# A new step order, engine choice and PSUM bank table for an RWKV-6 recurrence followed by a token-mixing MLP

## The chip, the cores and the metric

The kernel runs on one core of one Trainium2 chip. The metric is the device time of one execution in microseconds (us). Before the change three runs gave 100.65, 100.91 and 101.37 us, a median of 100.91 us.

## The reference

Shapes: batch 4, 8 heads, 768 tokens, 48 columns per head, so 384 model columns; 64 hidden columns in the mixer. Inputs and output are float32.

```python
for t in range(S):                                   # for each of 4 x 8 heads
    y[:, :, t] = r_t @ (state + (u * k_t) (x) v_t)   # (x): outer product, 48 x 48
    state = w_t[:, None] * state + k_t (x) v_t
x = y as [B, S, H * D]
W_tok = (x @ w_q) @ (x @ w_k).T / 8                  # per batch, 768 x 768, no softmax
out = relu(W_tok @ x) @ w_out
```

The kernel never forms `W_tok`: it forms T = (x w_k)^T x (64 x 384) once per batch and multiplies by (x w_q), so the mixer of a batch waits for all of that batch's tokens.

## The kernel before

**Units.** The work is cut into 12 units of 256 tokens (three per batch, n = 0 to 11), each of two chunks c = 0, 1 of 128 tokens. `unit` (L382) adds the steps of one unit to a plan. For each unit four loads of 384 KB (`wg`, `kg`, `rg`, `vg`; for the last batch v comes in four loads `vw`) go through SyncE's queue into rings of four buffers. Unit n, by the names used below, in order of dependence:

- `ln` (L407, ScalarE): log of w; `cw`: its running sum, on TensorE; `ep`, `en` (L447, L454, ScalarE): exponentials of it, read from the same PSUM buffer.
- `k16`, `r16`, `v16` (L418, L421, L543): casts to bf16; `kT`, `rT`: transposes on TensorE into one PSUM buffer of two banks; `ks` (L502): copy of the transposed k; `qT` (L506), `RT` (L516): products read from the transposed r, always on VectorE; `KT` (L519): from `ks` and `en` on GpSimd (way P), from the same on VectorE (D), or from the PSUM buffer and `en` on VectorE (d).
- `vp`, `VB` (L555): v in the chunk's row order; for the last batch `VB` is a copy from `vw` (L537). `dps`, `dd`: the bonus with u; `Vd` (L575, GpSimd) = VB times dd.
- `A` (TensorE) and `AM` (L595, VectorE, one per chunk): masked scores; `kb`, `kd`: k by rows; `sn` (TensorE) and `SB` (L658, VectorE): the state, passed from chunk to chunk.
- `yi`, `ya` (TensorE): the state's and the scores' part of y; `X` (L710, in the last unit L715, VectorE): y plus Vd, the mixer's input; `xt`, `XT`: its transpose; `qk`, `QK`: the hidden columns. The last unit does this by chunk (`wq`, `wk`).
- After a batch's third unit: `T`, `TS`; then for each of the three units `mx` (TensorE), `rl` (relu into tile MX, L339 or L341), `fp` (TensorE, w_out), `os` (copy to an output tile, L327 or L333), `st` (store, SyncE's queue L841).

In the profile nearly all copies have line L327 (ScalarE) or L333 (VectorE, GpSimd), scaled ones L329 or L335, and every matmul has line L179. A step on TensorE is a run of 3 to 16 pairs of one weight load and one matmul.

**What sets the order.** Nothing is scheduled at run time. Three tables at the top of the file decide: `ORDER` (L82) gives the sequence in which the 734 steps are written out, and so each engine's own instruction order; `WAYS` (L124) gives one letter for each step that has a choice of engine or form (P GpSimd, D or d VectorE, A ScalarE; E, e, c forms on TensorE); `BANKS` (L129) gives the first of the eight PSUM banks for each PSUM buffer. `Plan.order` (L61) applies them. Each engine runs its steps strictly in that order and waits by semaphores for what a step reads, for the buffer it overwrites, and, where VectorE and ScalarE read the same PSUM banks, for the reader that was written out first. Twelve `z` steps are idle matmuls on zeros, also placed by the table.

Of the kernel before, what the change touches and what calls it, by code (L numbers as in the profile page):

```python
# [32 lines left out]
class Plan:  # L33
# [46 lines left out]


ORDER = [  # L82
# [40 lines left out]
]  # L123
WAYS = (  # L124
    "PDDDAPPDDdPADPPDDEEEAAPPAdPAAPEAcEEAAPPAPPADPeDEEDAAAAAAAAPPDPDADPeAcEEDAPPAdPAAPEAEEEDA"
    "PPDPPAAPeAEEAAAAAAAAAAPDPPAAPEDEcEAAPPDPPDAPEAEEEAAPPDPPAAPeDceAAAAADADDPAAPPAPEDcEEDAPP"
    "DPPAPeAcceAAPPDPPPAPPAEEDDAEDADAAADAAAADADDA"
)
BANKS = [  # L129
# [6 lines left out]
]  # L136


# [755 lines left out]
```

## Time and profile before

| | |
|---|---|
| median of 3 runs | 100.91 us (100.65 to 101.37) |
| span of the profiled execution | 99.6 us |
| median less span | 1.31 us |
| VectorE busy | 84.9 us of the span |
| ScalarE busy | 79.0 us |
| TensorE matmul busy | 86.6 us |
| GpSimd busy | 69.5 us |
| read from HBM, written | 19.66 MB, 4.72 MB |

The profiled execution is known by its span alone, the time from its first to its last recorded instruction; what lies around the span is taken as the 1.31 us between it and the median. Busy times are of instructions that run; matmuls overlap, so a busy TensorE is not one at its peak. In rows of the timeline the first number is the start, the second the duration, and a bracket at the end gives the idle time before the row and what ended it. "issue" as the thing that ended a wait means that no semaphore did.

### The profile page before, as it was taken

Reading aid. Unit: us, or ns where it says so; the run is one execution under the profiler, and the core shown is the slowest. Engines: PE = TensorE matmul, PEld = TensorE weight load, DVE = VectorE, ACT = ScalarE, POOL = GpSimd, SP = SyncE. Lnnn points to the kernel's source line nnn. Section 1 sums busy time; section 2 is a strip of 40 time slices with the busy share of each in tenths; the row PEclk is TensorE's granted clock in tenths of the full one; section 3 lists DMA queues with packets and bytes.
Section 4 is the critical chain, followed back from the end, with each engine's and each line's share of the span. In section 5 each row is a group of like instructions: output and inputs, shape, how many; then the busy total and the mean of one; then the engine's idle time right before and its main releaser. Section 6 shows DMA issues by size and latency. Waiting matters only on the chain.

```text
span 99.6 us, 4492 instructions
## 1 busy us (share of the span) xinstructions
PE 86.6 (87%) x1906; PEld 63.3 (64%) x1911; DVE 84.9 (85%) x154; ACT 79.0 (79%) x135; POOL 69.5 (70%) x82
## 2 busy tenths in 40 slices
PE   5978796879886998999999999889998999999930
PEld 1325473756774767777776777759787687776610
DVE  6284999799979999979999999999999799783740
ACT  6034998799996799899999998999899766666920
POOL 6866354999799895799999989498996392500000
PEclk9999999999999999999999999999999999999999
DMA  1999999799999999999999977998993056030794
GB/s 17 313 327 349 324 337 296 195 295 335 289 314 298 225 311 329 344 321 268 271 330 305 316 114 218 251 156 201 282 417 115 7 210 264 10 158 7 277 367 149
DMA packets 45141, 24.68 MB, mean 248 GB/s; under 512 B 31552, under 2 KB 43968, under 8 KB 45120
## 3 DMA queue, kind: packets, MB, share of 16 engines
q1 hardware_dynamic: 44960, 24.19, 84.0%
q8 instruction: 15, 0.25, 0.9%
q10 hardware_dynamic: 160, 0.20, 0.5%
q14 instruction: 6, 0.05, 0.1%
HBM read 19.66 MB, written 4.72 MB: 245 GB/s over the span
## 4 chain that ended last, share of the span: by engine, by line
PE 37%; DVE 23%; SPq 20%; DMA 7%; issue 7%; ACT 3%; ACTq 0%; DVEq 0%
PE PS L179 37%; SPq L232 9%; SPq L237 8%; DMA vg<-in_v_dram 7%; DVE AM L595 7%; DVE X L710 6%; DVE RT L516 3%; SPq L355 2%; DVE qT L506 2%; DVE ks L333 2%; DVE SB L658 1%; ACT VB L327 1%; SPq L357 1%; ACT MX L339 1%; DVE kd L335 1%
## 5 line engine op out<-in xcount | busy, mean ns | idle before, releaser
L595 DVE TENSOR_TENSOR AM<-PS,US 128x1024 bf16<-128x1024 f32 x24 | 28.8, 1218 | 0.7 <-PE PS L179 0.7
L526 POOL TENSOR_TENSOR KT<-ks,en 128x1024 bf16<-128x1024 bf16 (+1 forms) x10 | 19.7, 1965 | 4.7 <-DVE ks L333 3.3
L575 POOL TENSOR_TENSOR Vd<-VB,dd 128x768 bf16<-128x768 bf16 (+1 forms) x14 | 18.1, 1293 | 4.5 <-ACT dd L327 3.4
L454 ACT ACTIVATE en<-PS 128x1024 bf16<-128x1024 f32 (+1 forms) x14 | 12.5, 907 | 3.0 <-PE PS L179 2.9
L179 PEld LDWEIGHTS <-KT 48*128 48x128 bf16 (+1 forms) x312 | 9.7, 94 | 6.6 <-issue 4.5
L447 ACT ACTIVATE ep<-PS 128x512 bf16<-128x512 f32 (+1 forms) x28 | 13.7, 555 | 0.1
L179 PE MATMUL PS<-wo,MX 128*128 128x384 bf16 x72 | 13.5, 327 | 0.0
L710 DVE SCALAR_TENSOR_TENSOR X<-PS,gx,Vd 128x384 bf16<-128x384 f32 x22 | 12.5, 609 | 0.7 <-PE PS L179 0.6
L407 ACT ACTIVATE lw<-wg 128x768 bf16<-128x768 f32 x12 | 10.3, 857 | 2.9 <-DMA wg<-in_w_dram 2.9
L179 PE MATMUL PS<-RT,KT 48*128 48x128 bf16 x192 | 9.7, 218 | 1.2 <-ACT VB L327 0.4
L327 ACT COPY os<-PS 128x768 f32<-128x768 f32 (+1 forms) x11 | 7.9, 714 | 3.5 <-PE PS L179 3.5
L418 POOL CAST k<-kg 128x768 bf16<-128x768 f32 x10 | 8.3, 827 | 2.5 <-DMA kg<-in_k_dram 2.5
L179 PE MATMUL PS<-Z 128*128 128x512 bf16 x25 | 8.4, 461 | 1.4 <-DVE Z L250 1.2
L418 POOL CAST r<-rg 128x768 bf16<-128x768 f32 x10 | 8.2, 825 | 1.6 <-DMA rg<-in_r_dram 1.6
L179 PEld LDWEIGHTS <-MX 128*128 128x128 bf16 x72 | 6.5, 97 | 3.6 <-DVE MX L341 0.2
L516 DVE TENSOR_TENSOR RT<-PS,ep 128x1024 bf16<-128x1024 bf16 (+1 forms) x14 | 8.4, 605 | 0.0
L179 PE MATMUL PS<-VB,AM 128*128 128x48 bf16 x192 | 8.0, 184 | 0.4 <-issue 0.4
L506 DVE TENSOR_TENSOR qT<-PS,ks 128x1024 bf16<-128x1024 bf16 x12 | 8.2, 684 | 0.1
L339 ACT ACTIVATE MX<-PS 128x768 bf16<-128x768 f32 (+1 forms) x12 | 8.0, 682 | 0.4
L179 PE MATMUL PS<-CM,lw 64*128 64x128 bf16 x192 | 7.4, 217 | 0.5 <-DVE AM L595 0.3
L327 ACT CAST VB<-PS 128x768 bf16<-128x768 f32 x8 | 6.4, 804 | 1.1 <-PE PS L179 0.6
L179 PEld LDWEIGHTS <-AM 128*128 128x128 bf16 x192 | 6.3, 96 | 1.6 <-issue 0.7
(90 smaller groups left out, 191.9 us busy)
## 6 DMA issues: line engine op xcount, KB each, us to landing
kg<-in_k_dram SPq DMA_DIRECT2D x12, 384.0 KB, 6.4
wg<-in_w_dram SPq DMA_DIRECT2D x12, 384.0 KB, 5.0
rg<-in_r_dram SPq DMA_DIRECT2D x12, 384.0 KB, 5.8
vg<-in_v_dram SPq DMA_DIRECT2D x9, 384.0 KB, 6.3
out_dram<-os SPq DMA_DIRECT2D x9, 384.0 KB, 2.5
vw<-in_v_dram SPq DMA_DIRECT2D x4, 288.0 KB, 6.7
out_dram<-os SPq DMA_DIRECT2D x5, 192.0 KB, 2.4
wof<-in_moe_w_out_dram SPq DMA_DIRECT2D x1, 576.0 KB, 6.2
```

Of the source, the lines that this page charges most:

```text
L179: return nc.tensor.matmul(o, l, rr, start=start, stop=stop, skip_group_check=True, is_transpose=trans)
L327: nc.scalar.copy(o, i)
L407: nc.scalar.activation(view(lw.tile, 0, [[64, H], [512, 2], [1, D]]), view(g["wg"].tile, 0, [[D2, H], [D, 2], [1, D]]), ACT.Ln, bias=0.0, ...
L418: op(view(o.tile, 0, [[64, NP], [256, 4], [1, D]]), view(g[src].tile, 0, [[2 * D2, NP], [D, 4], [1, D]]))
L447: nc.scalar.activation(view(ep.tile, cs[0] * NP * EW + off, [[EW, NP * len(cs)], [step, 2], [1, 32]]), view(at(cw), cs[0] * 512 + j * 64, ...
L454: nc.scalar.activation(en.tile[:, ds(cs[0] * 512, w_)], at(cw)[:, ds(cs[0] * 512, w_)], ACT.Exp, bias=0.0, scale=-1.0)
L506: lambda e: nc.vector.tensor_tensor(plain(qT.tile), turned(512), plain(ks.tile), ALU.mult),
L516: nc.vector.tensor_tensor(plain(RT.tile, cs, 32), turned(512, cs, True), plain(ep.tile, cs, EW // 4), ALU.mult)
L526: x.tensor_tensor(KT.tile[:, cols], ks.tile[:, cols], en.tile[:, cols], ALU.mult)
L575: (nc.vector if e == "D" else nc.gpsimd).tensor_tensor(Vd.tile[:, cols], VB.tile[:, cols], view(dd.tile, cs[0] * H, [[1, len(cs) * H], [0, ...
L595: AMs[c] = add(("AM", n, c), "D", lambda e, c=c, A=A: nc.vector.tensor_tensor(view(AM[c].tile, 0, [[C, 8], [1, C]]), view(at(A), 0, [[C, 8 ...
L710: nc.vector.scalar_tensor_tensor(view(X.tile, 2 * i * DM + hh * D, [[D2, H], [1, D]]), view(at(y), hh * 512, [[D, H], [1, D]]), gx, view(V ...
```

## The change

Only the three tables change. The functions, the operations and their operands are the same, and the numbers of buffers too. The description that comes with it: the order was searched with a model that lets two readers of a PSUM bank take turns and that holds TensorE's instruction blocks apart.

```diff
 ORDER = [
-    0, 3, 13, 2, 21, 22, 23, 15, 16, 17, 1, 24, 25, 26, 27, 28, 29, 76, 77, 78, 31, 73, 74, 75,
...
+    0, 1, 2, 3, 4, 24, 25, 26, 15, 16, 17, 32, 30, 33, 21, 22, 23, 31, 38, 39, 730, 13, 18, 19,
...
 WAYS = (
-    "PDDDAPPDDdPADPPDDEEEAAPPAdPAAPEAcEEAAPPAPPADPeDEEDAAAAAAAAPPDPDADPeAcEEDAPPAdPAAPEAEEEDA"
...
+    "PPPAAADDdPPADPPDDEEeAAPPAdPADPEAccEAAPPDPPAAPeAcEAAAAAAAAAPPAdPAAPEAEEEDAPPDPPAAPEAEEEAA"
...
 BANKS = [
-    7, 2, 0, 6, 0, 6, 4, 4, 1, 1, 6, 6, 5, 4, 2, 6, 0, 0, 0, 7, 7, 6, 4, 5, 4, 4, 2, 2, 7, 0, 0,
...
+    5, 0, 2, 0, 2, 4, 2, 0, 3, 3, 4, 0, 7, 4, 6, 6, 7, 2, 4, 2, 5, 5, 6, 7, 5, 0, 2, 6, 1, 2, 0,
...
```

Steps that change engine or form, by unit:

- from VectorE: `pads` 0 and 1 (zeroing `kd`), `v16` 3 to GpSimd; `uC`, `ks` 3, `VB` 7, `XT` 2 and 4, `kd` 2, 8 and 9, `dd` 2 and 3, `rl` 7 and 8 and some `os` to ScalarE; `KT` 4 and the second half of `KT` 0 to GpSimd (the first half of `KT` 0 goes from form D to form d);
- to VectorE: `r16` 0, `KT` 3 and 6 and the first half of `KT` 11 from GpSimd; `ks` 2, 4 and 9, `kd` 5, 7 and 11, `dd` 1, 6 and 9, `XT` 8, `QK` 7 and 9, `TS` 8 and 11, `rl` 9 and a half of `rl` 10 from ScalarE;
- between GpSimd and ScalarE: `k16` 0, `r16` 5, `v16` 8 and `VB` 9 go to ScalarE, `k16` 6 and `r16` 9 to GpSimd;
- on TensorE: four `kb` steps take the form with half as many matmuls, so 1887 pairs stand in the program instead of 1911.

The first loads were kg 0, wg 0, rg 0, vg 0, kg 1, wg 1, rg 1, vg 1 and so on; now they are rg 0, wg 0, kg 0, kg 1, wg 1, rg 1, vg 0, kg 2, wg 2, vg 1, rg 2, vg 2. The two small loads of w_q and w_k stood 13th and now come after rg 4, 18th.

The moved pieces at three places follow. A name is a tile with the ring slot and a running number.

**VectorE at the start of the program** (units 0 and 1; KT_0, RT_0, ks_0, ep_0 are unit 0's). Before:

```order
L297 MEMSET kd_0_83 128x32
L298 MEMSET kd_0_83 128x16x40
L297 MEMSET kd_1_84 128x32
L298 MEMSET kd_1_84 128x16x40
L333 CAST uC_134<-uR_133 8x128
L333 COPY ks_0_95<-PS_62 128x1024
L526 TENSOR_TENSOR KT_0_101<-ks_0_95,en_0_93 128x512
L521 TENSOR_TENSOR KT_0_101<-PS_62,en_0_93 128x512
L516 TENSOR_TENSOR RT_0_99<-PS_62,ep_0_91 128x512
L506 TENSOR_TENSOR qT_0_97<-PS_62,ks_0_95 128x1024
```

Now:

```order
L421 CAST r16_0_87<-rg_0_67 128x8x2x48
L333 COPY ks_0_95<-PS_62 128x1024
L521 TENSOR_TENSOR KT_0_101<-PS_62,en_0_93 128x512
L516 TENSOR_TENSOR RT_0_99<-PS_62,ep_0_91 128x512
L506 TENSOR_TENSOR qT_0_97<-PS_62,ks_0_95 128x1024
L595 TENSOR_TENSOR AM0_0_111<-PS_62,US_146 128x1024
L516 TENSOR_TENSOR RT_0_99<-PS_62,ep_0_91 128x512
L333 COPY dd_0_107<-PS_62 128x16
L335 TENSOR_SCALAR kd_0_83<-PS_62,gk_152 128x8x48 x2
L595 TENSOR_TENSOR AM1_0_113<-PS_62,US_146 128x1024
```

The memsets and the cast of uC are gone from VectorE, the cast of r is there, and the first AM follows right behind the first chunk's KT, RT and qT, ahead of kd.

**ScalarE ahead of the last unit's `ln`** (lw_1_86 from wg_3_66 is unit 11's, kd_0_83 is unit 10's, XT_0_119 is unit 8's). Before:

```order
L327 COPY os_3_82<-PS_62 128x768
L327 COPY XT_0_119<-PS_62 128x768
L327 CAST QK_0_127<-PS_62 128x384
L329 ACTIVATE kd_0_83<-PS_62,gk_152 128x16x48
L327 CAST QK_0_127<-PS_62 128x384
L407 ACTIVATE lw_1_86<-wg_3_66 128x8x2x48
```

Now:

```order
L327 COPY os_3_82<-PS_62 128x768
L329 ACTIVATE kd_0_83<-PS_62,gk_152 128x16x48
L339 ACTIVATE MX_0_121<-PS_62 128x768
L327 COPY dd_0_107<-PS_62 128x16
L327 CAST VB_1_106<-vw_0_131 128x8x2x48
L339 ACTIVATE MX_1_122<-PS_62 128x768
L407 ACTIVATE lw_1_86<-wg_3_66 128x8x2x48
```

Unit 9's VB, which GpSimd made, now stands in ScalarE's row behind kd, MX and dd, and the state step `sn` 9 on TensorE and `SB` 9 on VectorE wait for it; XT 8 and one QK have left.

**ScalarE in the last batch's mixer** (os_2_81 is unit 6's output tile and os_3_82 unit 7's; XT_0_119 is unit 10's; MX_0_121 is unit 8's). Before:

```order
L327 COPY XT_0_119<-PS_62 128x768
L327 COPY os_2_81<-PS_62 128x768
L327 CAST QK_1_128<-PS_62 128x384 x2
L327 CAST QK_1_128<-PS_62 128x128
L327 CAST QK_1_128<-PS_62 128x64
L327 CAST TS_1_130<-PS_62 128x384
L327 COPY os_3_82<-PS_62 128x768
```

Now:

```order
L327 COPY XT_0_119<-PS_62 128x768
L327 COPY os_3_82<-PS_62 128x768
L327 CAST QK_1_128<-PS_62 128x64
L327 CAST QK_1_128<-PS_62 128x384
L339 ACTIVATE MX_0_121<-PS_62 128x768
L327 COPY os_0_79<-PS_62 128x768
```

Unit 7's output (fp 7 on TensorE, then os 7) now precedes the last T and TS; before it followed them. TS 11 is on VectorE now. On TensorE the end reads: fp 8, mx 9, mx 10, mx 11, then fp 9, and the halves of fp 11 and fp 10 by turns; before it read fp 7, mx 9, fp 8, mx 10, fp 9, mx 11, fp 10, fp 11.

More of the change, by code (lines that the diff above doesn't have):

```diff
@@ L82 @@
 ORDER = [
[40 rows of a table removed]
[40 rows of a table added]
 ]
 WAYS = (
-    "PDDDAPPDDdPADPPDDEEEAAPPAdPAAPEAcEEAAPPAPPADPeDEEDAAAAAAAAPPDPDADPeAcEEDAPPAdPAAPEAEEEDA"
-    "PPDPPAAPeAEEAAAAAAAAAAPDPPAAPEDEcEAAPPDPPDAPEAEEEAAPPDPPAAPeDceAAAAADADDPAAPPAPEDcEEDAPP"
-    "DPPAPeAcceAAPPDPPPAPPAEEDDAEDADAAADAAAADADDA"
+    "PPPAAADDdPPADPPDDEEeAAPPAdPADPEAccEAAPPDPPAAPeAcEAAAAAAAAAPPAdPAAPEAEEEDAPPDPPAAPEAEEEAA"
+    "PADPPAAPEDEEAAAAAAAAAPPDdPADPEDcEEAAPPDPPAAPEDEEEADPPDPAAAPEAEEDADAAAAAAPPDPADPEAccEDDPP"
+    "DPPAPEAcEeAAPPDdPPAPPDEEDADEDDDDDDADADDDADAA"
 )
 BANKS = [
[6 rows of a table removed]
[6 rows of a table added]
 ]
```

88 rows, old and new, of tables (BANKS, ORDER) are left out of this document.

## The prediction

> **What bounds the kernel now.** I read the page's busy shares first, then busy time by stretch, then the timelines of VectorE, TensorE, ScalarE and GpSimd around each idle time of VectorE.
>
> ```profile
> span 99.6 us, 4492 instructions
> DVE  6284999799979999979999999999999799783740
> DMA  1999999799999999999999977998993056030794
> q8 instruction: 15, 0.25, 0.9%
> ```
>
> ```profile
> 6.00:27.00 21.00, 16.99 (x417) 11.99 (x419) 18.78 (x37) 17.29 (x30) 14.65 (x16) 1.00 1.07 307
> 27.00:36.00 9.00, 7.74 (x204) 6.13 (x203) 8.27 (x15) 7.21 (x11) 8.44 (x8) 1.00 0.99 276
> 36.00:75.50 39.50, 37.67 (x961) 29.48 (x960) 38.76 (x61) 38.27 (x64) 35.46 (x31) 1.00 1.01 277
> 75.50:85.60 10.10, 9.43 (x216) 6.85 (x217) 9.21 (x17) 6.66 (x16) 5.71 (x7) 1.00 0.33 125
> 85.60:95.60 10.00, 9.96 (x107) 7.01 (x108) 6.70 (x13) 6.97 (x15) 0.52 (x1) 1.00 0.38 145
> ```
>
> The columns of the second view are TensorE, weight loads, VectorE, ScalarE, GpSimd, granted clock, DMA share and GB/s. From 6.0 to 85.6 us, where the last AM ends, VectorE is busy 18.78 + 8.27 + 38.76 + 9.21 = 75.0 of 79.6 us: it sets the pace and is idle 4.6 us. ScalarE is nearly as full in the long middle (38.27 of 39.5). Behind 85.6 the last unit's mixer is a chain with TensorE in the lead. DMA is full early, so the first 30 us also hang on when loads land. So the span is 6.0 + VectorE's work up to the last AM + its idle time + the chain behind it, and I cost the change by these terms.
>
> ```profile
> 83.23 2.34 DVE L595 TENSOR_TENSOR AM<-PS,US 128x1024 bf16<-128x1024 f32 x2
> 86.24 1.14 DVE L715 SCALAR_TENSOR_TENSOR X<-PS,gx,Vd 128x384 bf16<-128x384 f32 x2 [0.67 <-PE PS L179]
> 94.23 0.56 DVE L341 TENSOR_SCALAR MX<-PS 128x384 bf16<-128x384 f32 x1 [0.73 <-ACT MX L339]
> ```
>
> ```profile
> 93.70 0.50 ACT L339 ACTIVATE MX<-PS 128x384 bf16<-128x384 f32 x1
> ...
> 95.64 0.48 ACT L327 COPY os<-PS 128x384 f32<-128x384 f32 x1 [0.98 <-PE PS L179]
> ```
>
> The chain from AM's end (85.57) to the last copy's end (96.12) takes 10.55 us, the last store and the close 3.5 us: 6.0 + 75.0 + 4.6 + 10.5 + 3.5 = 99.6. The median of the runs is 1.31 us above this span, and I add the same 1.31 to mine.
>
> **The work that moves.** Nothing is removed but 24 of 1911 pairs on TensorE, which is not the pace. What counts is how much VectorE must do before the last AM.
>
> ```profile
> L333 DVE COPY ks<-PS 128x1024 bf16<-128x1024 bf16 x8 | 5.5, 685 | 1.7 <-PE PS L179 1.7
> L327 ACT COPY ks<-PS 128x1024 bf16<-128x1024 bf16 x4 | 4.0, 1008 | 1.1 <-PE PS L179 1.1
> L521 DVE TENSOR_TENSOR KT<-PS,en 128x1024 bf16<-128x1024 bf16 x2 | 1.4, 678 | 0.0
> L333 DVE CAST v<-vg 128x768 bf16<-128x768 f32 x1 | 1.3, 1306 | 0.7 <-DMA vg<-in_v_dram 0.7
> L327 ACT CAST VB<-PS 128x768 bf16<-128x768 f32 x8 | 6.4, 804 | 1.1 <-PE PS L179 0.6 <-issue 0.4
> ```
>
> In a full row an instruction costs about 0.08 us less than its mean, since the next starts that much before its end: 0.60 for ks or KT, 1.23 for the cast. Off VectorE: pads and uC 1.6 (they run from 6.00 to 7.59, uC last, row below), the v cast 1.23, ks 3 and KT 4 1.2, three kd 1.56, two XT 0.94, VB 7 0.86, KT 0 0.6, two dd 0.2: 8.2. Onto it: the r cast 1.23, three ks 1.8, KT 3 and 6 1.2, kd 5 and 7 1.04, XT 8, QK 7 and TS 8 1.38, halves of KT 11 and kd 11 0.66, three dd 0.3: 7.6. So VectorE has 0.6 us less: 74.4. ScalarE, by the same count, has 1.9 us more to do up to the end of `ln` 11 (63.0 for 61.1); GpSimd loses over 2 us in all and is no bound (35.46 of 39.5 in the middle).
>
> **The start.** VectorE's idle times before 10 us are 0.94 and 0.38, waits for kT 0 and for en 0.
>
> ```profile
> 6.16 0.59 DVE L298 MEMSET kd<- 128x640 uint32 x1
> 7.39 0.20 DVE L333 CAST uC<-uR 8x128 bf16<-8x128 f32 x1
> 8.52 0.69 DVE L333 COPY ks<-PS 128x1024 bf16<-128x1024 bf16 x1 [0.94 <-PE PS L179]
> 12.62 1.22 DVE L595 TENSOR_TENSOR AM<-PS,US 128x1024 bf16<-128x1024 f32 x1
> 19.32 1.14 DVE L710 SCALAR_TENSOR_TENSOR X<-PS,gx,Vd 128x384 bf16<-128x384 f32 x2 [0.62 <-PE PS L179]
> 28.62 1.31 DVE L333 CAST v<-vg 128x768 bf16<-128x768 f32 x1 [0.73 <-DMA vg<-in_v_dram]
> ```
>
> ```profile
> 6.69 0.83 POOL L421 CAST r<-rg 128x768 bf16<-128x768 f32 x1 [0.73 <-DMA rg<-in_r_dram]
> 9.17 0.83 POOL L418 CAST k<-kg 128x768 bf16<-128x768 f32 x1 [0.41 <-DMA kg<-in_k_dram]
> 11.55 0.83 POOL L418 CAST r<-rg 128x768 bf16<-128x768 f32 x1 [1.55 <-DMA rg<-in_r_dram]
> 38.16 1.15 POOL L333 CAST wo<-wof 128x1152 bf16<-128x1152 f32 x1 [0.60 <-DMA wof<-in_moe_w_out_dram]
> ```
>
> ```profile
> 8.96 1.08 ACT L454 ACTIVATE en<-PS 128x512 bf16<-128x512 f32 x2 [2.66 <-PE PS L179]
> ```
>
> The casts of r, k and r show that the 3rd, 5th and 7th load land at 6.7, 9.2 and 11.5 us. Now kg 0 is third: k16 on ScalarE 6.7 to 7.5, kT 0.4, ks at 8.0; cw 0 is first on TensorE, so en 0 follows k16 at 7.7 instead of 8.96. KT, RT and qT fill VectorE to 10.0, and A runs under qT: the first AM starts at 10.0 instead of 12.62, and its idle time here is about 0.7 instead of 1.3. vg 0 is now seventh, so v16 ends at 12.4, VB on ScalarE at 13.6 and the first state can be at 14.1; the second AM, dd, kd and KT 1 cover VectorE until then. How long GpSimd takes to zero kd the rows do not show: between VectorE's own 0.6 and the 1.15 of GpSimd's largest cast, twice; I take 0.85. The half of KT 0 behind it ends at 10.8, and its AM is due at 12.3, so either end is hidden.
>
> What is late next is GpSimd's and ScalarE's part of units 2 to 4. Nineteen loads and two small ones land by 28.6 (row of v above), 1.3 us each. On this pace, with the loads in their new order, r16 2 at 18 and KT 2 on GpSimd (2.1) to 21.4 make AM wait 0.5; KT 3, now read by VectorE from the PSUM buffer that ScalarE copies ks 3 from, waits for that copy until 26.3, 0.9; ks 4 waits for kg 4 behind wcast (the casts of w_q and w_k) and v16 in GpSimd's row, another 0.6. The 0.62 at 18.7 and 0.73 at 28.6 of before go. Up to 36 us before had 3.0 us of such idle time, now I count 0.7 + 0.5 + 0.9 + 0.6 = 2.7. If the later w_q load lets units 3 and 4 land a microsecond sooner it is 1.4; if each wait doubles, 4.5.
>
> That the second reader of a bank waits is what the row at 94.23 shows: MX of VectorE starts 0.03 us behind the ScalarE MX of the same buffer (0.50 from 93.70). [...]
>
> **TensorE's instruction blocks.** Some groups of matmuls break in the middle with no semaphore to wait for:
>
> ```profile
> 28.75 0.21 PE L179 MATMUL PS<-VB,AM 128*128 128x48 bf16 x2 [0.40 <-issue]
> 72.51 0.31 PE L179 MATMUL PS<-VB,kd 128*64 128x48 bf16 x8
> 77.34 0.29 PE L179 MATMUL PS<-PM,k 64*128 64x64 bf16 x8 [0.51 <-issue]
> ```
>
> ```profile
> 72.51:77.34 4.83, 4.32 (x128) 3.82 (x128) 4.72 (x8) 4.67 (x10) 3.89 (x5) 1.00 0.64 249
> ```
>
> ```profile
> 77.97 0.69 DVE L333 COPY ks<-PS 128x1024 bf16<-128x1024 bf16 x1 [0.74 <-PE PS L179]
> ```
>
> Two such breaks enclose exactly 128 pairs, and there are 15 instruction packets for 3822 instructions: TensorE's program comes in blocks of 256, and a block that is used up within some 4.8 us stands until the next has come. At 77.34 this made the last kT late, and VectorE waited 0.74. Counting pairs in the new order, that block runs from qk 7 to kT 11 again, but VectorE has 5.8 us of work between what goes with these (before 4.8 elapsed), so the break should be gone: minus 0.7. Closest now is A 4 to kT 6, with 4.4 us of VectorE's work between; if it breaks, 0.5 to 0.7 is lost there. [...]
>
> **ScalarE ahead of the last batch.**
>
> ```profile
> 74.67 0.85 ACT L407 ACTIVATE lw<-wg 128x768 bf16<-128x768 f32 x1
> ```
>
> VB 9 now stands two steps ahead of ln 11. With ScalarE's old idle time, ln 11 would end 1.9 later than 75.5; its earlier start in unit 0 (k16 at 6.7 instead of waiting 2.66) gives 2 back, and up to 1.5 more if the waits between 27 and 36 us (7.21 of 9.0 busy) go too, so VB 9 ends near 72.9, between 72.4 and 75.9. With sn 9 (0.5) behind it SB 9 starts at 73.4, while VectorE, at 6.0 + 62.2 of work + 3.6 idle, could at 71.8 to 72.4. I take a wait of 1.0.
>
> Idle time now: 2.7 + 1.0 + 0.9 for the small waits of the middle and the end (before: 4.6 - 3.0 - 0.74) = 4.6, as before. The last AM ends at 6.0 + 74.4 + 4.6 = 85.0.
>
> **The end.**
>
> ```profile
> 88.71 0.72 PE L179 MATMUL PS<-X,QK 128*64 128x384 bf16 x6
> 89.54 1.14 PE L179 MATMUL PS<-wo,MX 128*128 128x384 bf16 x6
> 93.45 2.11 PE L179 MATMUL PS<-wo,MX 128*128 128x384 bf16 x12
> ```
>
> Before, T (88.71) starts 3.1 behind the last AM; then fp 7 (89.54) and four more fp with three mx follow to 95.56. Now fp 7 (1.0) comes right behind ya, where TensorE waits for X; it makes xt 0.35 late, mx 7 and qk 9 are gone from there, and T ends 4.15 behind AM for 3.9. Behind T stand fp 8, three mx and three fp: 1.0 + 1.0 + 3.0 instead of 6.1. Part is lost again, because fp 11 takes fp 9's banks and waits for both halves of os 9 (0.15), rl 10 and rl 11 are read in turns by ScalarE and VectorE, and a VectorE copy (0.55) ends it. I get 10.0 from AM to the last copy, between 9.6 and 10.8.
>
> **Sum.** 85.0 + 10.0 + 3.5 = 98.5; with 1.31 that is 99.8, 1.1% under the median. A result within 1% of 100.91 (99.9 to 101.9) could hardly be told from no change.
>
> **Rivals.**
>
> *The start keeps its lead* (0.20). Loads land early enough that the waits at KT 2, KT 3 and ks 4 shrink to 0.7 in all and ScalarE is never late: idle 1.4 + 0.9 = 2.3, AM ends at 82.7, span 96.2, time 97.5. For it: the two small loads have left their place between the loads of units 2 and 3. Against: ScalarE's 1.9 us more.
>
> *ScalarE becomes the bound at VB 9* (0.14). If it idles as long as before, VB 9 ends at 75.9, SB 9 starts at 76.4, and VectorE still owes 11.4 of work up to the last AM: 87.8 + 0.3, span 101.6, time 102.9, slower by 2%. It decides from VB 9 at 72.4 on, microsecond by microsecond, and is slower by over 1% from 75.0. For it: 38.27 of 39.5 busy; against: the earlier start.
>
> *The gains are given back* (0.28). The block break comes back between A 4 and kT 6 (0.6) or at kT 11, and the turns at the end eat what fp 7 gave (0.5): 100.9. This is also what the change would give if it does not do what it says.
>
> The forecast itself has 0.38. Its own range is 99.0 to 100.6, about half of it under 99.9. Faster by over 1%: 0.20 + 0.6 of 0.38 + a little of the third = 0.46; slower: 0.14 + 0.04 = 0.18; same 0.36. From 97.5 to 102.0 takes in all but the worst part of the ScalarE case.
>
> **What would show it.** Right: first AM at 10.0, VectorE's first wait over 0.5 between 20 and 32 us, no break in kT 11, T about 3.4 to 4.2 behind the last AM, the last AM at 85.0. Wrong: VB 9 ending past 75 with VectorE waiting over 2 us for SB 9; or VectorE idle under 3 us up to the last AM, and then it is the first rival.

## The result and the profile after

| | before | changed |
|---|---|---|
| median, first comparison (21 runs each) | 101.29 us (100.49 to 104.42) | 101.09 us (99.29 to 102.90) |
| ratio, 95% interval | | 0.9891 (0.9849 to 0.9933) |
| second comparison, on one chip (30 and 12 runs) | 101.54 us | 101.54 us, ratio 0.9992 (0.9927 to 1.0057) |
| span of the profiled execution | 99.6 us | 100.6 us |
| median span of the unedited runs (58 and 33) | 99.95 us | 99.3 us |

Each ratio takes only the runs within 1.5% of the fastest run of the same kernel, in the first comparison 6 of the change's 21, while the quotient of the medians of all runs is 0.998 there and 1.000 in the second. The unedited runs of before come from three chips, and on the one chip where both kernels have spans the medians are 99.8 and 99.7. The profiled execution of the change happens to be one of its longer ones. So the gain is small, between nothing and 1.5%, and one kernel's own runs lie further apart (spans of 97.5 to 102.2 for the change) than the two kernels. The question became what makes up this spread, and what the order gains beneath it.

The page of the changed kernel:

```profile
span 100.6 us, 4438 instructions
DVE  6264999999999758989899999999989999975850
q8 instruction: 14, 0.23, 1.0%
```

VectorE is still full nearly throughout. The hole near 30 us is gone, and others stand between 32 and 45 us. By stretch up to the last AM (TensorE, weight loads, VectorE, ScalarE, GpSimd), first this execution, then one of the change with a single edit (VB 9 on GpSimd) and the shortest span of all unhalved profiles, 97.6:

```profile
6.00:87.53 81.53, 74.62 (x1788) 57.14 (x1787) 75.20 (x125) 70.45 (x118) 63.48 (x60) 1.00 0.94 261
```

```profile
6.00:84.26 78.26, 73.80 (x1785) 56.82 (x1784) 74.75 (x125) 69.87 (x117) 63.95 (x61) 1.00 0.95 270
```

VectorE does 75.2 or 74.75 us of work (75.02 before); its idle time, the stretch less this work, is 6.3 in the one and 3.5 in the other, against 4.6 before. VectorE's waits and TensorE's breaks in the first:

```profile
8.81 0.69 DVE L333 COPY ks<-PS 128x1024 bf16<-128x1024 bf16 x1 [1.91 <-PE PS L179]
10.84 1.23 DVE L595 TENSOR_TENSOR AM<-PS,US 128x1024 bf16<-128x1024 f32 x1
34.22 0.36 DVE L658 TENSOR_TENSOR SB<-PS,ep 128x192 bf16<-128x192 f32 x1 [0.58 <-PE PS L179]
36.82 0.69 DVE L333 COPY ks<-PS 128x1024 bf16<-128x1024 bf16 x1 [1.19 <-PE PS L179]
```

```profile
33.04 0.36 PE L179 MATMUL PS<-VB,AM 128*128 128x48 bf16 x8 [1.03 <-issue]
45.66 0.24 PE L179 MATMUL PS<-PM,k 64*128 64x64 bf16 x5 [0.78 <-issue]
79.39 0.40 PE L179 MATMUL PS<-PM,k 64*128 64x64 bf16 x16
```

The first AM is at 10.84, before it was 12.62, and the wait for kT 0 grew to 1.91. Last row: the 16 pairs of kT 11, which broke at 77.34 before, run through. In their place ya 3 breaks at 33.04 and kT 6 (behind A 4) at 45.66, at pairs 607 and 863 of TensorE's program: 256 pairs apart, two blocks. A place where TensorE passes from one block to the next is called a crossing below.

ScalarE and VectorE around VB 9, and then the end:

```profile
74.14 0.85 ACT L327 CAST VB<-vw 128x768 bf16<-128x768 f32 x1
```

```profile
74.61 0.55 DVE L333 COPY XT<-PS 128x768 bf16<-128x768 bf16 x1
75.08 0.55 DVE L333 CAST QK<-PS 128x384 bf16<-128x384 f32 x1
75.57 0.36 DVE L658 TENSOR_TENSOR SB<-PS,ep 128x192 bf16<-128x192 f32 x1
```

```profile
85.17 2.36 DVE L595 TENSOR_TENSOR AM<-PS,US 128x1024 bf16<-128x1024 f32 x2 [0.16 <-PE PS L179]
```

```profile
87.89 1.14 PE L179 MATMUL PS<-wo,MX 128*128 128x384 bf16 x6
90.72 0.81 PE L179 MATMUL PS<-X,QK 128*64 128x384 bf16 x6
```

```profile
97.04 0.56 DVE L333 COPY os<-PS 128x384 f32<-128x384 f32 x1 [0.49 <-PE PS L179]
```

VB 9 ends at 74.99 and SB 9 starts 0.6 behind it without idle time: XT 8 and QK 7 filled the gap. At the end the last AM stops at 87.53, fp 7 runs in TensorE's wait for X, T starts 3.19 behind AM, and the last copy ends 10.07 behind AM (10.55 before). From there to the end it is 3.0 us, before 3.5.

### The profile page after: what moved, and what is told of

It reads as the page before. It is cut to its first block, busy times and chain, and to the rows that moved or that the text cites. A ratio compares the mean times of both kernels' runs of the same rounds, so it can differ in the third digit from the quotient of the medians.

```text
span 100.6 us, 4438 instructions
## 1 busy us (share of the span) xinstructions
PE 88.8 (88%) x1887; PEld 64.7 (64%) x1887; DVE 85.3 (85%) x156; ACT 78.7 (78%) x132; POOL 68.2 (68%) x83
## 4 chain that ended last, share of the span: by engine, by line
PE 40%; DVE 25%; SPq 11%; issue 7%; DMA 6%; POOL 4%; ACT 3%; POOLq 0%; DVEq 0%
PE PS L179 40%; DVE AM L595 8%; SPq L237 6%; DMA vg<-in_v_dram 6%; SPq L232 5%; DVE X L710 5%; DVE qT L506 3%; DVE SB L658 2%; POOL KT L526 2%; DVE ks L333 2%; DVE RT L516 2%; POOL Vd L575 1%; ACT os L327 1%; DVE kd L335 1%; POOL k L418 1%
## 5 line engine op out<-in xcount | busy, mean ns | idle before, releaser
L526 POOL TENSOR_TENSOR KT<-ks,en 128x1024 bf16<-128x1024 bf16 (+1 forms) x9 | 17.2, 1912 | 4.5 <-DVE ks L333 3.4
L179 PEld LDWEIGHTS <-KT 48*128 48x128 bf16 (+1 forms) x288 | 10.7, 94 | 4.7 <-issue 3.3
L327 ACT COPY os<-PS 128x768 f32<-128x768 f32 (+1 forms) x12 | 8.6, 720 | 6.1 <-PE PS L179 4.0
L418 POOL CAST k<-kg 128x768 bf16<-128x768 f32 x11 | 9.1, 825 | 4.9 <-DMA kg<-in_k_dram 4.7
L179 PE MATMUL PS<-Z 128*128 128x512 bf16 x30 | 10.4, 477 | 2.0 <-DVE Z L250 1.2
L333 DVE COPY ks<-PS 128x1024 bf16<-128x1024 bf16 x10 | 6.9, 686 | 3.3 <-PE PS L179 3.3
L179 PE MATMUL PS<-VB,AM 128*128 128x48 bf16 x192 | 7.3, 184 | 1.0 <-issue 1.0
L658 DVE TENSOR_TENSOR SB<-PS,ep 128x192 bf16<-128x192 f32 x20 | 7.1, 354 | 1.2 <-PE PS L179 0.8
```

What stands on the lines that cost most here:

```text
L179: return nc.tensor.matmul(o, l, rr, start=start, stop=stop, skip_group_check=True, is_transpose=trans)
L327: nc.scalar.copy(o, i)
L418: op(view(o.tile, 0, [[64, NP], [256, 4], [1, D]]), view(g[src].tile, 0, [[2 * D2, NP], [D, 4], [1, D]]))
L526: x.tensor_tensor(KT.tile[:, cols], ks.tile[:, cols], en.tile[:, cols], ALU.mult)
```

## The experiments

The theory behind them: VectorE sets the pace, and what moves the time is when TensorE delivers, which at two places hangs on something no semaphore shows, the start of TensorE's program and its instruction blocks. The rival: ScalarE's queue (VB 9) and the loads decide.

**The change again, unedited** (a1_change_again), as the base of the first four.

> The changed kernel itself, for a second profile beside the first (span 100.6 us). Theory: the median ratio to the kernel before is again 0.985 to 0.993; the last AM ends 85 to 87 us after the start and the last copy of the output 10.0 us behind it, as in the first profile; breaks of TensorE's stream without a semaphore fall at the same two pair numbers (607 and 863 of the weight loads). Rival: the gain comes and goes with the place of the loads in time, so that the idle time of VectorE up to the last AM differs by over 1.5 us between the two profiles.

Median 101.54 us, ratio 0.9992 (0.9927 to 1.0057), above the 0.985 to 0.993 that was expected. In its profile (span 99.8) the first AM starts at 11.35, kT 6 breaks for 0.92 us, and ya 3 doesn't break. Same program, same pair numbers, other waits. VectorE's idle time is 5.7 us instead of 6.3, a smaller difference than the rival asked for.

**Fewer zero matmuls at the start** (a2_warmup_12).

```diff
-        for _ in range(18):
+        for _ in range(12):
             mm(PS[:, ds(0, 512)], Z[:, ds(0, C)], Z)
```

> The changed kernel with 12 instead of 18 matmuls on zeros ahead of the work (nothing of the result is left out). Theory: in the changed kernel those matmuls hold TensorE until 7.7 us, though the first running sum could start at 6.2, and so cause 1.2 of VectorE's 1.9 us wait before its first copy of k; with 12 they end near 6.3, the first AM starts at 10.0 instead of 10.84, and the time falls by 0.5 to 1 us (0.5 to 1%). Rival: the loads of units 2 to 5 set the pace of the first 35 us, so an earlier first AM is given back there and the time stays within 0.3%. Third possibility: fewer matmuls leave TensorE slow for longer, and the first AM comes no earlier.

100.93 us, ratio 0.9987 (0.9929 to 1.0044). TensorE at the start, of the change and of this kernel:

```profile
2.49 5.25 PE L179 MATMUL PS<-Z 128*128 128x512 bf16 x15
7.68 0.62 PE L179 MATMUL PS<-CM,lw 64*128 64x128 bf16 x16
8.13 0.40 PE L179 MATMUL PS<-PM,k 64*128 64x64 bf16 x16
```

```profile
6.30 0.62 PE L179 MATMUL PS<-CM,lw 64*128 64x128 bf16 x16
7.49 0.41 PE L179 MATMUL PS<-PM,k 64*128 64x64 bf16 x16 [0.57 <-ACT k L421]
```

The log of w is ready at 6.1 to 6.4, but cw 0 waits for the zeros until 7.68; with 12 it starts at 6.30, and then k16 on ScalarE holds kT 0. The zeros follow each other at 0.427 us until some moment and at 0.216 after it; the last long step started at 4.62 us in the profiles of before and of the VB 9 edit, at 5.05, 5.91 and 7.19 in three others of this order. So the first AM of this order falls between 10.2 and 11.4 from one execution to the next, and with 12 zeros at 10.26. The time shows no difference that this comparison could tell.

**VB 9 back on GpSimd** (a3_vb9_gpsimd): one letter in the table of ways.

```diff
-    "PADPPAAPEDEEAAAAAAAAAPPDdPADPEDcEEAAPPDPPAAPEDEEEADPPDPAAAPEAEEDADAAAAAAPPDPADPEAccEDDPP"
+    "PADPPAAPEDEEAAAAAAAAAPPDdPADPEDcEEAAPPDPPAAPEDEEEADPPDPAAAPEAEEDADAAAAAAPPDPPDPEAccEDDPP"
```

> The changed kernel with VB of unit 9 back on GpSimd. The forecast's theory: ScalarE makes VectorE wait about 1.0 us for that step, so the time falls by 0.5 to 1 us. Rival, from the first profile after the change, where VectorE has other copies to do until VB 9 is there and shows no wait at the state step of unit 9: nothing is won (within 0.3%), and only GpSimd's 2.5 us wait ahead of its product Vd 9 goes.

100.80 us, ratio 0.9965 (0.992 to 1.0011). Around SB 9 nothing changes for VectorE: XT 8, QK 7 and SB 9 follow each other as above (71.34, 71.80, 72.29). Its profile is the shortest; it has an early start (first AM at 10.22) and crossings of 0.25 and 0.27 us at most. VB 9's engine is not a bound of VectorE. Behind the last copy, though, the four profiles with VB 9 on GpSimd take 3.3 us and most others of this order 3.0; why stays open.

**fp 7 behind T again** (a4_fp7_late): steps 514 (fp 7), 515 (os 7) and its store.

```diff
-    664, 621, 622, 666, 580, 665, 667, 509, 510, 511, 514, 668, 623, 674, 675, 515, 669, 676,
+    664, 621, 622, 666, 580, 665, 667, 509, 510, 511, 668, 623, 674, 675, 669, 676, 670, 356,
...
+    357, 358, 519, 672, 671, 678, 677, 624, 681, 682, 679, 683, 514, 680, 684, 520, 515, 516,
```

> The changed kernel with unit 7's last product, its copy and its store put back behind the last batch's T (ahead of fp 8), as the kernel before had it. Theory: this undoes what shortens the end, the last copy comes 10.5 to 11 us behind the last AM instead of 10.0, and the time rises by 0.5 to 1 us. Rival: TensorE waits there anyway, and the end is as long with it as without (within 0.2 us).

102.55 us, ratio 1.0135 (1.0045 to 1.0226), against 0.9992 (0.9927 to 1.0057) for the change on the same chip.

```profile
89.34 0.81 PE L179 MATMUL PS<-X,QK 128*64 128x384 bf16 x6
90.08 2.12 PE L179 MATMUL PS<-wo,MX 128*128 128x384 bf16 x12
```

The last AM ends at 86.17, so T starts 3.17 behind it, as with fp 7 ahead of it; behind T now stand 12 pairs of fp in a row, and the last copy ends 11.03 behind AM instead of 10.07. fp 7's place is worth 0.96 us, all of it behind T.

**The block crossings moved** (b1_blocks_shifted): 32 more pairs ahead of the program.

```diff
-        for _ in range(18):
+        for _ in range(14):
             mm(PS[:, ds(0, 512)], Z[:, ds(0, C)], Z)
+        for _ in range(36):
+            mm(PS[:, ds(0, 8)], Z[:, ds(0, C)], Z[:, ds(0, 8)])
```

> The changed kernel with the warm-up before unit 0 made of 14 long and 36 very short zero matmuls instead of 18 long ones: 32 more pairs stand in TensorE's program ahead of everything, and nothing else moves. Theory (blocks of 256 instructions, counted from the program's start): breaks without a semaphore still start at pair numbers 95 + 128 k (607, 863), which are now other steps; the step from A 4 to kT 6, whose pair 863 stood 0.92 to 1.12 us in three profiled executions of the unshifted order, now holds pairs around 895 and does not break; the total changes by the breaks that the new sites get, between -1.0 and +0.5 us. Rival (the stall belongs to the step, a wait that the profile does not name): the break stays in the matmuls of A 4 to kT 6, at pair 895 or so, and the time is that of the unshifted order.

101.03 us, ratio 0.9967 (0.9909 to 1.0025). kT 6, and for comparison the same step in the kernel of the experiment after next, which leaves the crossings where the change has them:

```profile
44.42 0.41 PE L179 MATMUL PS<-PM,k 64*128 64x64 bf16 x16
```

```profile
42.79 0.34 PE L179 MATMUL PS<-PM,k 64*128 64x64 bf16 x11
44.71 0.24 PE L179 MATMUL PS<-PM,k 64*128 64x64 bf16 x5 [1.57 <-issue]
```

Moved by 32 pairs, the step runs through. A break stands at another pair of the same count, 735, in the middle of a `wq`:

```profile
37.32 0.49 PE L179 MATMUL PS<-XT,wq 128*128 128x256 bf16 x3 [0.31 <-issue]
```

From one weight load to the next this crossing takes 0.51 us, the others at most 0.20. So the break belongs to the pair number, not to the step. The time didn't follow: the six spans are 98.8 to 99.6, with a median of 99.35 against 99.3 for the change. In its profile VectorE lost 1.7 us elsewhere, in two waits between 21 and 25 us, the second of them where the granted clock had fallen (last section).

**Half of the data** (b2_half_loads): from unit 4 on each load of w, k, r and v moves four of eight heads. The output is not the reference's, since the other half of each buffer is left from an earlier unit.

```diff
+        hh = H if b * NU + i < 4 else H // 2
         nc.sync.dma_start(
-            out=view(tl, 0, [[D2, H], [1, D2]]),
-            in_=ap[b, :, ds(i * U, U)].rearrange("h (p j) d -> p h (j d)", j=2))
+            out=view(tl, 0, [[D2, hh], [1, D2]]),
+            in_=ap[b, ds(0, hh), ds(i * U, U)].rearrange("h (p j) d -> p h (j d)", j=2))
```

> The changed kernel with loads of w, k, r and v that move only half of the heads from unit 4 on (the other half of each buffer keeps what an earlier unit left there, so the output is not the reference's; every engine does the same work). Theory (TensorE's next instruction block comes late because its packet queues behind data): past 35 us the packets start within 0.6 us of the crossing, no break over 0.2 us is left from there, VectorE's idle time up to the last AM falls to 2.5 to 3.5 us, the last AM ends by 84.5, the span is 97 to 98 and the median about 1.5 us under the unchanged order's on this chip. Rival (a block takes its time to come whatever else moves): the packets start 1.5 to 3.5 us after the crossing as before, and breaks of 0.3 to 1.1 us stay at pair 863.

99.77 us, ratio 0.9854 (0.9797 to 0.9911), and all six spans within 97.4 to 97.9. That is a narrow spread, though the shifted kernel above had only 0.8 us in six runs at full load. From 35 to 80 us no crossing takes over 0.06 us. Instruction packets are not as prompt as expected (0.2 to 2.3 us behind the crossing there, not 0.6), but early enough. VectorE's idle time is 3.85 us, above the expected 2.5 to 3.5.

**The small loads early** (b3_small_loads_early): w_q and w_k 13th again (their issue and the two land steps, 5 to 7, stand behind unit 2's last load).

```diff
-    146, 109, 145, 110, 192, 193, 194, 147, 148, 149, 111, 150, 144, 204, 195, 196, 197, 112,
+    5, 6, 7, 146, 109, 145, 110, 192, 193, 194, 147, 148, 149, 111, 150, 144, 204, 195, 196,
...
-    254, 5, 6, 7, 162, 159, 161, 118, 8, 212, 201, 202, 203, 215, 257, 226, 213, 243, 244, 245,
+    247, 248, 254, 162, 159, 161, 118, 8, 212, 201, 202, 203, 215, 257, 226, 213, 243, 244, 245,
```

> The changed kernel with the two small loads of w_q and w_k (and the small wait steps that go with them) issued directly behind unit 2's last load, 13th, as in the kernel before, instead of 18th. Theory (loads bound the first 35 us, and the later place of these two is one of the things that the change gains): the loads of units 3 and 4 land 0.5 to 1.0 us later, VectorE's idle time between 18 and 38 us grows by about as much, the time by 0.3 to 0.9 us. Rival (this stretch is bound by GpSimd and ScalarE, the loads wait for a free buffer anyway): within 0.3 us of the unchanged order.

101.82 us, ratio 0.9887 (0.9779 to 0.9996), too wide to tell by time. Its profile has one wait of VectorE over 0.2 us between 18 and 38 us, of 0.26 at KT 3, and the change itself has more there; this profile gives no support to the theory that the later place gains anything. (This is the kernel with the 1.57 row above.)

**12 zeros and VB 9 together** (b4_warmup12_vb9).

> The changed kernel with both single edits that looked no worse alone: 12 zero matmuls instead of 18 before unit 0, and VB 9 on GpSimd as in the kernel before. Theory (TensorE is free when the first running sum is due, and ScalarE's queue ahead of the last batch is 0.7 shorter): first AM at 10.2, last AM between 84.0 and 85.5, span 97.5 to 98.5, the median about 0.6 us under the kernel before, 0.994. Rival (both only shift when the block breaks fall): the ratio to the kernel before is 0.999, that of the unchanged order on the same chip as before.

100.69 us against 102.14 for the kernel before on that chip, ratio 0.993 (0.9865 to 0.9994), six spans of 98.5 to 99.2. First AM at 10.13, the end of the last AM at 85.16. The median of the spans is 98.95, against 99.3 for the change, but the two are not separated.

**Both orders with half of the data, on one chip** (c1_before_half_loads, c2_after_half_loads; the loads as in b2, so these outputs are not the reference's either).

> The kernel before with loads that move only half of the heads from unit 4 on (the other half of each buffer is left from an earlier unit, so the output is not the reference's; the work of the engines is unchanged). With little data on the way the spread from late instruction blocks should be gone, so this against the next run shows what the new order is worth without it. Theory (the order gains 0.5 at the end, by fp 7, and 0.3 to 0.7 before the last AM; the rest of what single executions show is blocks): no break over 0.3 us past 40 us, spans of 98.3 to 99.0, 0.8 to 1.2 us over the changed order with the same loads. Rival (most of the gain is that the new order meets fewer or shorter breaks): spans within 0.5 us of the changed order's.

> The changed kernel with the same halved loads from unit 4 on (output not the reference's), again, on the chip of the run before this one. Expected: spans of 97.4 to 97.9, all runs within 0.8 us, as before; packets of instructions within 0.7 us of the crossing past 42 us.

99.64 and 99.52 us, ratios to the kernel before 0.9893 (0.9827 to 0.9958) and 0.9876 (0.9819 to 0.9933); profiled spans 97.8 and 97.7. The medians of the spans are 97.9 and 97.55, so the two orders differ by 0.1 to 0.35 us, as the rival had it and not by the 0.8 to 1.2 of the theory. The spread does not go away in both: the changed order's spans are 97.4 to 97.9 again, those of the order before 97.7 to 99.6, the two longest, 99.0 and 99.6, at mean clocks of 0.978 and 0.964. The packets of the changed order start up to 1.6 us behind a crossing, not within the expected 0.7, and its times lie 1.07 us apart, not 0.8. Up to the last AM, before and changed:

```profile
6.00:83.76 77.76, 71.96 (x1791) 54.19 (x1789) 74.86 (x125) 69.00 (x117) 64.08 (x59) 1.00 0.71 198
```

```profile
6.00:84.58 78.58, 74.19 (x1788) 56.98 (x1787) 74.56 (x125) 70.69 (x118) 62.97 (x60) 1.00 0.72 198
```

The changed order has 0.3 less work on VectorE (74.86 to 74.56) but 1.1 more idle time (2.9 to 4.0), and reaches the last AM 0.82 later; behind it the copies end at 10.07 instead of 10.55, the close takes 3.0 instead of 3.5, together 0.96 back. The largest part of the loss is one row, its wait for kT 0 (0.94 for the same tile in the order before):

```profile
9.11 0.69 DVE L335 COPY ks<-PS 128x1024 bf16<-128x1024 bf16 x1 [2.22 <-PE PS L179]
```

Halving the loads takes more away than late instruction blocks: before, VectorE waited 0.73 us at 28.62 for `vg` to land, and in the order before with halved loads the same cast starts at 27.65 without a wait. The new order has no such wait at full load either, so this comparison hides what it gains there.

**The same with 12 zeros and VB 9 on GpSimd** (c3_half_loads_warmup12_vb9; output again not the reference's).

> The changed kernel with halved loads from unit 4 on (output not the reference's), 12 zero matmuls instead of 18 and VB 9 on GpSimd. Theory (TensorE's zeros hold up the first running sum by 0.3 to 1.4 us from run to run, and VectorE, which sets the pace, never gets this back): median 0.3 to 0.6 under the changed order with halved loads, from the first AM at 10.1; VB 9 adds nothing, since VectorE had other work there. Rival (loads catch up with an early start within the first 30 us, so the start is worth nothing): within 0.2 us.

99.35 us, ratio 0.9881 (0.9811 to 0.9951). Its wait for kT 0 is 1.44 instead of 2.22, and its last AM stops at 84.06 instead of 84.58: 0.5 of the first AM's lead of 0.8 is kept. But the medians of the times differ by 0.17 and those of the spans by 0.05, within the 0.2 of the rival: in time the earlier start is not shown to be worth anything.

**The version meant to be best** (c4_shift_warmup10_vb9): VB 9 on GpSimd as above, and

```diff
-        for _ in range(18):
+        for _ in range(10):
             mm(PS[:, ds(0, 512)], Z[:, ds(0, C)], Z)
+        for _ in range(40):
+            mm(PS[:, ds(0, 8)], Z[:, ds(0, C)], Z[:, ds(0, 8)])
```

> The changed kernel with all its loads, with 10 long and 40 very short zero matmuls in place of 18 long ones (32 more pairs, so that the block crossings stand where the shifted run had no break over 0.2 us), and VB 9 on GpSimd as before the change: the version meant to beat both. Theory (blocks, start): first AM at 10.1 to 10.5, no break over 0.3 us, last AM by 85, spans of 97.7 to 98.8, ratio to the kernel before 0.987. Rival (late packets only find other steps to stop): spans as the version with 12 zero matmuls, 98.5 to 99.2, ratio 0.993.

101.53 us, ratio 1.0021 (0.9966 to 1.0076): no gain, and spans of 98.8 to 101.3, longer than theory and rival both had. No crossing takes over 0.26 us, as expected, but the start is late:

```profile
6.66 1.04 PE L179 MATMUL PS<-CM,lw 64*128 64x128 bf16 x16
7.54 0.61 PE L179 MATMUL PS<-PM,k 64*128 64x64 bf16 x16
```

```profile
11.34 1.22 DVE L597 TENSOR_TENSOR AM<-PS,US 128x1024 bf16<-128x1024 f32 x1 [0.77 <-PE PS L179]
```

Running sum and transposes take 1.04 and 0.61 us instead of 0.62 and 0.40: TensorE is still at its slow pace when unit 0 needs it. It had not been at full pace before either: its ten long zeros all went at 0.427 us a step, and in the trace the record of its clock begins only at 10.13 (last section).

## Why the prediction was right, and where it was not

**The time.** The measured 101.09 lies within the stated 97.5 to 102.0, but outside the forecast's own 99.0 to 100.6. 99.8 against a median of 100.91 was a ratio of 0.989, which is the first comparison's; the second gave 0.999, and the medians of all runs 0.998 and 1.000. In microseconds the sum was too low: a span of 98.5, where the median span is 99.3, and 1.31 around the span, where most runs have 1.7 to 1.9. The base was one profiled execution that wasn't the one of the median. Of the 33 unedited runs of the change 10 have 2.2 to 2.6 around the span, of the 58 before none over 1.84; so part of what the spans gain is lost outside them, and why stays open. By time the result is nearest to the third rival, *the gains are given back* (100.9): its break between A 4 and kT 6 came, its loss at the end didn't.

Against the profiled 100.6 the sum's 98.5 was short by 0.8 of work, 1.7 of idle time and 0.1 behind the last AM, and long by 0.5 in the close. That the idle time of 4.6 lies within the 3.5 to 6.3 of the full-load profiles is luck: of its parts 2.0 for KT 2, KT 3 and ks 4 and 1.0 for VB 9 were not there, or nearly so, and a longer wait at the start and breaks of the blocks stood in their place.

**What bounds.** Right. From 6.0 to the last AM's end VectorE is busy 92 to 96% of the time in every full-load profile of this order, and the chain behind it has one length per order (10.07 or 10.08 with fp 7 in its new place, 10.55 before).

**VectorE's work.** Mis-sized: 0.6 less was predicted, and the full-load profiles of this order have between 0.3 less and 0.4 more. It was not the r cast: it took 1.55 where 1.31 was assumed, but it started at 5.34, so only 0.9 of it falls behind 6.0, where the sum begins and counted 1.23. The largest miss is a row that didn't move: the 20 SB take 0.5 to 0.6 more of VectorE's time (5.34 before, 5.96 in the changed kernel's profile), because 13 or 14 of them, not 19, start clearly before the instruction ahead has ended. The sum's 0.08 for this overlap held in a full row, and the new order leaves small gaps ahead of SB.

**The start.** The first AM's 10.0 nearly holds when TensorE is free in time (10.13 to 10.38 with 12 zeros, or with 18 where cw 0 started by 7.22). The step that failed is "cw 0 is first on TensorE, so en 0 follows k16 at 7.7": in the new order unit 0 wants TensorE at 6.1 to 6.4, and the 18 zeros hold it until 6.9 to 8.2. The idle time is 1.3 to 2.4, not 0.7. The first rival, which keeps the start's lead with an idle time of 2.3, didn't come true: 3.5 was the least at full load. (Zeroing kd took GpSimd 1.17 us, just over its upper bound of 1.15, and was hidden.)

**KT 2, KT 3, ks 4.** The predicted waits of 0.5, 0.9 and 0.6 aren't there: no wait over 0.2 us between 15 and 32 us in the profile of the change. KT 3 shows the turn-taking in three others, where ScalarE's copy of the same buffer was just ahead: 0.19 us in the VB 9 edit, 0.26 with the small loads early, and 0.50 with 12 zeros and VB 9 together. The first and the last:

```profile
26.16 0.69 DVE L521 TENSOR_TENSOR KT<-PS,en 128x1024 bf16<-128x1024 bf16 x1 [0.19 <-ACT ks L327]
```

```profile
26.56 0.69 DVE L521 TENSOR_TENSOR KT<-PS,en 128x1024 bf16<-128x1024 bf16 x1 [0.50 <-ACT ks L327]
```

So KT 3 came behind ScalarE's copy each time, as forecast, and the loss is 0.50 at most of the 0.9: in all twelve profiles of the new order KT 3 starts 0.03 to 0.11 us behind the end of that copy, and in the changed kernel's VectorE, late from the start, reaches KT 3 at 26.39, when the copy is done. What the start loses is not lost a second time here. The other way round, an early start can be given back here: the earliest first AM (10.13) has the 0.50, and its KT 3 starts later than that of the changed kernel with its first AM at 10.84.

**The blocks.** Right that the break in kT 11 would go (3 to 50 ns at that crossing in the unshifted profiles) and that A 4 to kT 6 was closest: from one weight load to the next its crossing took 0.92, 1.00, 1.12 and 1.79 us in four full-load profiles, 0.16 to 0.34 in three (in the two of these with 12 zeros it lies six pairs later in the order), 0.03 in the two with halved loads and 18 zeros. Predicted was 0.5 to 0.7 if it breaks, in a rival with 0.28; it should have been in the forecast, with a break at ya 3 as well. That a block stands when it is used up within some 4.8 us was an estimate from one row: in the change's profile a block whose weight loads run from 26.57 to 31.83 (5.3 us) ends in the break at ya 3, and one from 57.46 to 62.41 (5.0 us) in none; their packets started 4.1 and 1.4 us behind the crossing.

**VB 9.** It does come late on ScalarE (it ends at 74.99, past the 72.9 of the forecast, in an execution whose last AM ended 2.5 later than forecast), but the 1.0 of waiting is not there: VectorE had XT 8 and QK 7 to do. The rival in which ScalarE becomes the bound falls with that row: SB 9 waits for nothing, and with VB 9 on GpSimd it stands in the same place.

**The end.** Right, 10.07 for 10.0, and in its parts: T ends 4.00 behind the last AM where 4.15 was forecast (3.86 before), and from there to the last copy it is 6.07 for 5.85. Only that fp 7 would make T later is not seen: with fp 7 behind T again, T ends 3.98 behind AM. The close is 0.5 shorter than was assumed to carry over.

**Where the gain comes from.** With halved loads the new order gains 0.96 us behind the last AM and loses 0.82 before it. With full loads its median span is 0.65 lower over all chips, and 0.1 on the chip where both ran, so it is open whether there is more to explain. If there is, the blocks (the break at kT 11 gone, others come), the wait for `vg` that is gone and the clock below fit the profiles; with one full-load profile of the kernel before none of them is shown.

## What to carry to other kernels

When runs of one program differ by more than the change is worth, find what differs between their profiles first: here matmul groups that break with no semaphore where TensorE passes from one block of 128 pairs to the next, at full load for up to 1.79 us. An order that is tuned on one such trace tunes against chance. Halving the loads takes these breaks out (0.15 us at most between 35 and 80 us in the order before, 0.06 in the changed one), but a wait for data with them (0.73 us for `vg`), so it doesn't by itself show what the order is worth at full load. And idle matmuls ahead of the work are work in TensorE's queue: whoever moves the first real matmul forward has to shorten them with it (18 of them held cw 0 until 7.68 us, behind 12 it started at 6.30), and then has to see whether TensorE is still slow when the real work starts: behind 10 long and 40 short ones cw 0 took 1.04 us instead of 0.62.

## What the runs showed of the hardware

**Late instruction packets.** After TensorE passes a crossing, the next packet of 16 KB on queue q8 starts this much later, and where TensorE reaches the next crossing too early, it stands until 1.3 to 1.7 us behind that packet's end:

| kernel | crossing to start of packet, from 35 to 80 us | longest crossing there |
|---|---|---|
| before | 0.9 to 3.7 us | 0.70 us |
| changed | 0.4 to 3.6 us | 1.00 us |
| small loads early | 0.4 to 4.3 us | 1.79 us |
| before, halved loads | 0.2 to 1.6 us | 0.15 us |
| changed, halved loads | 0.3 to 1.6 us | 0.06 us |

One crossing of the order before is left out of the last column: there a weight load stands 0.31 us behind the one before it with full and with halved loads alike, and the matmuls have no idle time.

**The pace of the zeros.** How long the zeros go at 0.427 us a step varies by 3.0 us between profiles (the last long step starts at 4.20 to 7.19). The views print a granted clock of 1.00 for this time too, but the trace holds no record of the clock there: its first record begins at 4.56 to 7.25 us in the profiles with 18 zeros, where the pace changes (at 7.25 for the step at 7.19). With 12 zeros and VB 9 together it begins at 6.98, in the middle of the first running sum, whose matmuls come in twos every 0.107 us before it and every 0.056 us after. With 10 long and 40 short zeros it begins at 10.13. Later records, where a profile has them, follow at multiples of 3.41 us (95.57 long in the profiles of before and of the change; 17.07, 3.41 and 71.68 long with 12 zeros). What ends the slow pace is not shown.

**A clock that falls later.** In three of the profiled executions of the changed order (12 zeros, shifted blocks, halved loads) the granted clock drops to half after 22 us, and returns: 0.50 from 24 to 26 us with 12 zeros, 0.50 from 24 to 28 with shifted blocks, 0.57 from 24 to 26 with halved loads, and 1.00 again from 28, 30 and 26 us. Here the shifted kernel; the last three columns are granted clock, DMA share and GB/s:

```profile
18.00:22.00 4.00, 2.69 (x79) 2.18 (x77) 3.26 (x6) 3.10 (x5) 2.51 (x3) 1.00 1.02 291
22.00:29.00 7.00, 6.58 (x157) 5.76 (x151) 6.02 (x9) 5.66 (x10) 7.00 (x7) 0.54 0.93 261
29.00:33.00 4.00, 3.75 (x94) 2.93 (x92) 4.00 (x6) 3.99 (x8) 2.88 (x6) 0.95 1.06 315
```

A mean clock below 0.97 over the whole span was recorded in 20 of 58 unedited executions of the kernel before (median span 100.6, against 99.5 in the 32 at 0.99 or more), and in 3 of 33 of the change. In the halved loads a mean of 0.98 cost the changed order nothing (spans of 97.4 to 97.9 at 0.979 to 0.982 and at 0.994 to 1.0 alike), while the order before had its two longest spans, 99.0 and 99.6, at 0.978 and 0.964. What sets it off stays open, and so does whether the lower clock makes those runs longer.
